# A planner that serializes the readers of one PSUM bank, with new leads for its transfers, in a linear attention joined to a gated MLP

## The chip, the cores and the metric

The kernel runs on one core of a Trainium2 chip. The core has five engines with a queue of instructions each: TensorE (PE in the rows; its weight loads are PEld), VectorE (DVE), ScalarE (ACT), GpSimd (POOL) and SyncE (SP), which here only starts DMA transfers. The metric is the device time of one execution in microseconds (us), the median of several.

## The reference

Two stages follow each other. For 4 batches, 8 heads, 768 steps and head size 48:

```python
for t in range(S):
    cur = einsum('bhd,bhe->bhde', u * k[t], v[t])
    y[t] = einsum('bhd,bhde->bhe', r[t], state + cur)
    state = w[t][..., None] * state + einsum('bhd,bhe->bhde', k[t], v[t])
# x = y as (3072 tokens, 384)
h = x @ w_in                       # 384 -> 2048
g = h if h >= 1, 0 if h <= -1, (h + 1)**2 / 4 between
out = g @ w_out                    # 2048 -> 384
```

All arrays are 32-bit floats.

## The kernel before, in words

The 3072 tokens are 12 units `u` of 256 tokens, and 6 blocks of two units (512 tokens). A unit's recurrence is done in chunks of 64 steps: VectorE scans the products of `w` forward (`p`, line 434) and backward (`y`, line 429), scales `r` and `k` with them, TensorE multiplies `r` with `k` inside the chunks (`among`, line 483), VectorE takes the wanted triangle of each product out of its PSUM bank with a mask (`picked`, line 489), TensorE transposes `k` (`ktrans`, line 522, into a bank that the masks must have left), forms the state updates (`umat`, line 544), VectorE adds them up (line 562), and TensorE forms the output in two PSUM banks, one for each half `g` of the unit (`cross` and `along`, line 593). From these banks the unit's `x` is taken in a high and a low part: ScalarE copies the high part (line 650), VectorE subtracts it from the bank to get the low part (line 648), first of three quarters (`x`), then of the last quarter (`last`), which six small DMAs then spread over free rows of `x` (`fill`, line 692). A unit of the first block takes its low part in another way (TensorE subtracts the high part in the bank, ScalarE copies what is left, line 646). For units from the fifth on, GpSimd makes the product of `r` and `k` of the diagonal (line 501) from a tile `nk` that has a transfer of its own.

The MLP runs over 16 slices `f` of 128 hidden columns for each block; the 16 slices' first 5 (block 0) or 11 (block 1) are done for each unit apart, so that they can start when one unit is there. A step is `product_in` (9 matmuls, line 944, into one of two banks `h`), the gate (ScalarE lines 755, 756 and 759, VectorE lines 757 and 760) and `product_out` (9 matmuls, line 964, added up in three banks `acc`). Weights come as raw bits (`wraw`), one transfer of 768 KB for each slice, and are decoded once: ScalarE (lines 355, 358), GpSimd (line 359, into the one buffer `rr`), VectorE (line 361), ScalarE for the high part (line 351), VectorE for the low part (line 364). At the end of a block the `acc` banks are copied out and stored. For each piece of `w` ScalarE also does two passes (`guard`, lines 711 and 712), whose result decides whether a general fallback runs; for the first six units `w` is loaded a second time for that, into `fl`.

What sets the order of everything is a planner in the kernel. Each operation is an entry with engine, cost, what it reads and writes, and a due time; `Plan.order` places the entries one after the other on the engines by these costs, and the instructions are emitted in that order. An attention unit or a weight decode is a group, whose entries are due a lead (`LEADS`, `DECODES`) plus `SLACK` times its remaining path ahead of the step that needs it. Each engine runs its queue strictly in the emitted order. Where the plan sees TensorE idle for over 0.5 us, `kept_warm` adds matmuls of zeros (line 326) for 0.72 of that gap.

The framework below adds its own waits between emitted instructions that touch the same tile on different engines.

Of the kernel before, what the change touches and what calls it, by code (L numbers as in the profile page):

```python
# [48 lines left out]
class Plan:  # L49
# [19 lines left out]
    def add(self, engine, cost, emit, due, reads=(), writes=(), port=False, size=0, fresh=True, mode=128):  # L69
        deps = {self.writer[x] for x in (*reads, *writes) if x in self.writer}  # L70
        for x in writes:
            deps.update(self.readers.get(x, ()))
        n = len(self.ops)
        for x in reads:
            self.readers.setdefault(x, []).append(n)
        for x in writes:
# [3 lines left out]
                             fresh=fresh and engine == "PE", touch={*reads, *writes}, mode=mode))  # L80
        return n

    def group(self, first, when, lead):

        tail = {}
        for n in reversed(range(first, len(self.ops))):
# [3 lines left out]
            op["due"] = when, lead + SLACK * tail[n]  # L90
# [39 lines left out]
    def order(self):  # L130
# [26 lines left out]
        while any(open_.values()):  # L157
# [57 lines left out]
SLACK = 1.384  # L215
LEADS = {0: 200.34, 1: 17.94, 2: 10.1, 3: 21.34, 4: 40.45, 5: 51.11, 6: 84.54, 7: 119.23, 8: 114.23, 9: 96.67, 10: 78.32, 11: 100.22}
DECODES = [58.08, 65.33, 175.35, 38.53, 1.42, 5.14, 81.19, 4.4, 14.07, 65.02, 61.72, 84.69, 39.36, 203.15, 25.09, -1.54]
LEAD = 15
# [12 lines left out]
STEP, FIRST, PACED, AFTER = 27.1568, 703.402, 25.4941, 4.9  # L231
# [3 lines left out]
def attention_moe(tc, a):  # L235
# [56 lines left out]
    def load(due, out, in_, writes, reads=()):  # L292
        size = 4
        for x in out.shape:
            size *= x
        return op("SP", 0.45, due, reads, writes, lambda: nc.sync.dma_start(out=out, in_=in_), size=size)
# [41 lines left out]
    def weight(f, when):  # L338
# [27 lines left out]
        plan.group(first, when, DECODES[f])  # L366
# [12 lines left out]
    def attention(u, when):  # L379
# [323 lines left out]
        plan.group(first, when, LEADS.get(u, LEAD))  # L703
# [33 lines left out]
    def products(n):  # L737
# [14 lines left out]
        op("PE", 0.16 + 2.11 * k, due, [("wh", f), ("wl", f), *xs], [("b", 6 + hk)],  # L752
# [13 lines left out]
        for terms in LAST if done else [TERMS]:  # L766
            op("PE", 0.16 + 2.11 * k * len(terms) / 9, due, [("gh", gk), ("gl", gk), ("wh", f), ("wl", f)],
# [38 lines left out]
    for n in range(2 * GUARDED):  # L806
# [3 lines left out]
        load(due, w, a["w"][u, q][:, 0:SEG], [("fl", n % 2)])  # L810
# [223 lines left out]
```

## Time and profile before

| | us |
|---|---|
| median of 3 runs (lowest, highest) | 514.54 (513.45, 517.81) |
| the profiled execution | 515.29 |
| its span, first to last instruction | 513.5 |
| PE busy | 495.0 (96% of the span) |
| DVE busy | 335.5 (65%) |
| ACT busy | 296.4 (58%) |
| POOL busy | 103.1 (20%) |
| DMA queue of SP | 53.21 MB, 30.5% of 16 engines |

The profiled execution is 1.8 us longer than its span. Busy time counts a matmul of zeros as work, and a matmul at a low clock as more work, so the 96% is no measure of what is left to gain; that is read from single stretches.

### The profile page before, as it was taken

Reading aid. Unit: us, or ns where it says so; the run is one execution under the profiler, and the core shown is the slowest. Engines: PE = TensorE matmul, PEld = TensorE weight load, DVE = VectorE, ACT = ScalarE, POOL = GpSimd, SP = SyncE. Lnnn points to the kernel's source line nnn. Section 1 sums busy time; section 2 is a strip of 40 time slices with the busy share of each in tenths; the row PEclk is TensorE's granted clock in tenths of the full one; section 3 lists DMA queues with packets and bytes.
Section 4 is the critical chain, followed back from the end, with each engine's and each line's share of the span. In section 5 each row is a group of like instructions: output and inputs, shape, how many; then the busy total and the mean of one; then the engine's idle time right before and its main releaser. Section 6 shows DMA issues by size and latency. Waiting matters only on the chain.

```text
span 513.5 us, 13078 instructions
## 1 busy us (share of the span) xinstructions
PE 495.0 (96%) x5558; PEld 414.1 (81%) x5558; DVE 335.5 (65%) x561; ACT 296.4 (58%) x604; POOL 103.1 (20%) x68
## 2 busy tenths in 40 slices
PE   8898999998999999999999999999999999999993
PEld 7778988786999987787888888888878888888883
DVE  7699997878997969799987567334552333333331
ACT  3478799968874665555556456443463444544441
POOL 2468858721022131112111020000100000000000
PEclk9899999998999999999999999999999999999997
DMA  8955644065751453264342050000120000100002
GB/s 319 391 217 206 213 176 173 2 225 171 235 144 64 152 191 103 76 220 144 91 135 82 21 182 6 1 0 3 57 75 6 0 1 1 63 0 0 1 0 68
DMA packets 21921, 54.11 MB, mean 105 GB/s; under 512 B 3104, under 2 KB 8672, under 8 KB 21856
## 3 DMA queue, kind: packets, MB, share of 16 engines
q1 hardware_dynamic: 21856, 53.21, 30.5%
q8 instruction: 45, 0.74, 0.6%
q14 instruction: 20, 0.16, 0.1%
HBM read 46.32 MB, written 4.72 MB: 99 GB/s over the span
## 4 chain that ended last, share of the span: by engine, by line
PE 70%; DVE 11%; ACT 6%; POOL 6%; issue 5%; DMA 2%; SPq 0%; POOLq 0%; DVEq 0%
PE acc L964 30%; PE h L944 29%; POOL rr L359 5%; PE bank L593 3%; PE bank L483 2%; DVE g L757 1%; PE bank L544 1%; PE bank L326 1%; PE bank L522 1%; DVE gl L760 1%; ACT g L756 1%; DVE fl L361 1%; DVE p L434 1%; DVE rk L463 1%; DVE rk L513 1%
## 5 line engine op out<-in xcount | busy, mean ns | idle before, releaser
L944 PE MATMUL h<-x,wt 128*128 128x512 f32 (+1 forms) x1008 | 216.2, 361 | 1.0 <-DMA x<-last 0.7
L944 PEld LDWEIGHTS h<-x,wt 128*128 128x128 f32 x1008 | 168.9, 188 | 30.7 <-DVE g L757 1.3
L964 PE MATMUL acc<-gh,wt 128*128 128x512 f32 (+1 forms) x672 | 153.1, 362 | 0.0
L964 PEld LDWEIGHTS acc<-gh,wt 128*128 128x128 f32 x672 | 113.8, 188 | 18.7
L757 DVE SCALAR_TENSOR_TENSOR g<-g,h 128x512 f32<-128x512 f32 (+1 forms) x112 | 67.8, 606 | 90.3 <-ACT g L756 86.3
L755 ACT ACTIVATE g<-h 128x512 f32<-128x512 f32 (+1 forms) x112 | 59.8, 534 | 79.2 <-PE h L944 73.9
L760 DVE TENSOR_TENSOR gl<-g,gh 128x512 fp32r<-128x512 f32 (+1 forms) x112 | 74.5, 667 | 36.6 <-ACT gh L759 35.6
L759 ACT CAST gh<-g 128x512 fp32r<-128x512 f32 (+1 forms) x112 | 62.1, 556 | 50.1 <-DVE g L757 49.3
L964 PE MATMUL acc<-gl,wt 128*128 128x512 f32 (+1 forms) x336 | 84.5, 359 | 0.0
L964 PEld LDWEIGHTS acc<-gl,wt 128*128 128x128 f32 x336 | 58.9, 189 | 9.7
L756 ACT ACTIVATE g<-g 128x512 f32<-128x512 f32 (+1 forms) x112 | 64.0, 571 | 3.2
L359 POOL TENSOR_SCALAR rr<-wraw 128x768 uint16<-128x768 f32 x16 | 53.3, 3331 | 33.6 <-DVE fl L361 20.4
L509 POOL TENSOR_TENSOR r<-cst,d 128x512 f32<-128x512 f32 x16 | 19.3, 1227 | 155.3 <-PE bank L593 126.5
L434 DVE TENSOR_TENSOR_SCAN p<-wq,seeds 128x514 f32<-128x514 f32 x24 | 33.0, 1373 | 4.1 <-POOL st L313 2.1
L429 DVE TENSOR_TENSOR_SCAN y<-wq,seeds 128x514 f32<-128x514 f32 x24 | 30.0, 1251 | 0.8
L501 POOL TENSOR_TENSOR nk<-nk 128x768 f32<-128x768 f32 x8 | 15.7, 1961 | 62.7 <-DMA nk<-in_nk 62.7
L463 DVE TENSOR_TENSOR rk<-rk,y 128x512 f32<-128x512 f32 x24 | 18.1, 755 | 5.9 <-ACT nk L454 3.1
L529 ACT COPY kt<-bank 128x512 f32<-128x512 f32 x24 | 14.0, 582 | 12.5 <-PE bank L522 12.5
L358 ACT ACTIVATE rr<-wraw 128x768 uint16<-128x768 uint32 x16 | 17.5, 1092 | 1.7 <-DMA wraw<-in_wbits 0.9
L326 PE MATMUL bank<-clear 128*128 128x512 f32 (+1 forms) x53 | 16.4, 431 | 1.6 <-DVE seeds L433 1.6
L513 DVE TENSOR_TENSOR rk<-rk,p 128x512 f32<-128x512 f32 x24 | 17.7, 751 | 0.2 <-PE acc L483 0.2
L593 PEld LDWEIGHTS bank<-rk,st 48*48 48x48 f32 (+1 forms) x656 | 11.5, 121 | 7.6 <-DVE st L562 2.2
(109 smaller groups left out, 393.6 us busy)
## 6 DMA issues: line engine op xcount, KB each, us to landing
rk<-in_rk SPq DMA_DIRECT2D x24, 512.0 KB, 5.3
wraw<-in_wbits SPq DMA_DIRECT2D x16, 768.0 KB, 7.1
wq<-in_w SPq DMA_DIRECT2D x24, 257.5 KB, 3.0
nk<-in_nk SPq DMA_DIRECT2D x8, 768.0 KB, 4.4
vn<-in_v SPq DMA_DIRECT2D x11, 384.0 KB, 6.0
fl<-in_w SPq DMA_DIRECT2D x12, 257.0 KB, 3.5
out_y<-g SPq DMA_DIRECT2D x11, 256.0 KB, 2.6
x<-last SPq DMA_DIRECT2D x66, 32.0 KB, 2.9
```

Of the source, the lines that this page charges most:

```text
L359: op("POOL", 3.35, due, [("raw", f)], ["rr_high"], lambda: G.tensor_scalar(out=r16[:, :, 1], in0=wraw[f][:, :, 1].bitcast(F32), scalar1=0. ...
L429: V.tensor_tensor_scan(out=y_[:, ::-1], data0=w[:, SEG:0:-1], data1=sv[:, ::-1], initial=0.0, op0=ALU.mult, op1=ALU.add)
L434: V.tensor_tensor_scan(out=pv[:, q].rearrange("p n c -> p (n c)"), data0=w[:, 0:SEG], data1=sv, initial=0.0, op0=ALU.mult, op1=ALU.add,)
L463: op("DVE", 0.69, due, ["y"], [("k", s)], lambda q=q: V.tensor_tensor(out=parts(q, 1), in0=parts(q, 1), in1=y_.rearrange("p (n c) -> p n c ...
L593: PE.matmul(out=bank[by[g]][HP * half : HP * half + wide, lo : lo + C], start=first, stop=False, skip_group_check=True, **kw)
L755: op("ACT", c, due, [("b", 6 + hk)], [("g", gk)], lambda: nc.scalar.activation(gs, hs, AF.Relu, scale=0.5, bias=0.5))
L756: op("ACT", c, due, (), [("g", gk)], lambda: nc.scalar.activation(gs, gs, AF.Square))
L757: op("DVE", 0.13 + 0.56 * k, due, [("b", 6 + hk)], [("g", gk)], lambda: nc.vector.scalar_tensor_tensor(out=gs, in0=gs, scalar=1.0, in1=hs, ...
L759: op("ACT", c, due, [("g", gk)], [("gh", gk)], lambda: nc.scalar.copy(ghs, gs))
L760: op("DVE", 0.18 + 0.52 * k, due, [("g", gk), ("gh", gk)], [("gl", gk)], lambda: nc.vector.tensor_tensor(out=gls, in0=gs, in1=ghs.bitcast( ...
L944: nc.tensor.matmul(by16(hp, f), lhsT=wx[f][:, cs], rhs=by16(xt[:, j, :], f), start=n == 0, stop=n == 8)
L964: nc.tensor.matmul(by16(o[j]), lhsT=wx[f][:, cs], rhs=by16(gt), start=first and i == 0, stop=stop and i == 2, skip_group_check=True)
```

## The change

Six things change. A reader of a PSUM bank now depends, in the plan, on all earlier readers of that bank on other engines. In the evacuation of `x`, ScalarE's copies of all high parts of a bank are planned first, and VectorE's low parts after them. Transfers over 32 KB of a group get a lead of their own, added to that of the group (`LOADS`, `RAWS`). The planned arrival of the second loads of `w` for the guards is 2.5 us later. The planned costs of a whole step's matmuls fall from 2.11 to 2.04. The tables and constants (`SLACK`, `LEADS`, `DECODES`, `AFTER`) have new values, and with all of this the order of nearly every queue is another one. No operation is added or removed except matmuls of zeros (55 matmul widths of 512 columns before, 58.5 now, counted in the order).

```diff
@@ Plan.add
+        for x in reads:
+            if isinstance(x, tuple) and x[0] == "b":
+                deps.update(m for m in self.readers.get(x, ()) if self.ops[m]["e"] != engine)
@@ Plan.group
-            op["due"] = when, lead + SLACK * tail[n]
+            op["due"] = when, lead + SLACK * tail[n] + (loads if op["e"] == "SP" and op["size"] > 32768 else 0.0)
@@ Plan.order
                 lands.append(end[n])
+                end[n] += op["spare"]
@@
-SLACK = 1.384
-LEADS = {0: 200.34, 1: 17.94, 2: 10.1, 3: 21.34, 4: 40.45, ...
+SLACK = 0.759
+LEADS = {0: 384.81, 1: 606.87, 2: 40.05, 3: 27.03, 4: 45.45, ...
+LOADS = {0: 9.57, 1: -384.0, 2: -5.47, 3: 9.66, 4: 7.78, ...
-STEP, FIRST, PACED, AFTER = 27.1568, 703.402, 25.4941, 4.9
+STEP, FIRST, PACED, AFTER = 27.1568, 703.402, 25.4941, 8.52
@@ weight
-        plan.group(first, when, DECODES[f])
+        plan.group(first, when, DECODES[f], RAWS[f])
@@ attention
-        for what in (0,) if alone else (1, 0):
+        whats = (0,) if alone else (1, 0)
+        for g in range(2):
+            for what in whats:
+                op("ACT", 0.27 if what else 0.48, due, [("b", by[g])], [names(what, 0, g)], lambda g=g, w=what: yevac(g, 0, w))
+        if u not in INPLACE:
             for g in range(2):
-                op("ACT", 0.27 if what else 0.48, due, [("b", by[g])], [names(what, 0, g)], lambda g=g, w=what: yevac(g, 0, w))
-                if u not in INPLACE:
+                for what in whats:
                     op("DVE", 0.27 if what else 0.54, due, [("b", by[g]), names(what, 0, g)], [names(what, 1, g)],
                        lambda g=g, w=what: yevac(g, 1, w))
@@ products
-        op("PE", 0.16 + 2.11 * k, due, [("wh", f), ("wl", f), *xs], [("b", 6 + hk)],
+        op("PE", 0.16 + (2.04 if f and k == 1.0 else 2.11) * k, due, [("wh", f), ("wl", f), *xs], [("b", 6 + hk)],
@@ second loads of w
-        load(due, w, a["w"][u, q][:, 0:SEG], [("fl", n % 2)])
+        load(due, w, a["w"][u, q][:, 0:SEG], [("fl", n % 2)], spare=2.5)
```

What the new order is like is seen at three places. The first is ScalarE's queue in the start, from the copies of the transposed `k` of unit 0 on; `look` and the copies `g<-acc` and `x<-acc` are unit 0's evacuation, `wraw`, `fl`, `rr` and `wt` belong to the decode of weights, `ptot<-p` and `nk<-rk` to unit 1. Before:

```order
L529 COPY kt_93<-bank_123 128x512
L355 ACTIVATE fl_115<-wraw_218 128x768
L629 COPY look_76<-acc_117 1x1
L629 COPY look_76<-acc_118 1x1
L358 ACTIVATE rr_116<-wraw_220 128x768
L673 COPY g_106<-acc_117 128x128
L673 COPY g_106<-acc_118 128x128
L355 ACTIVATE fl_114<-wraw_220 128x768
L460 COPY ptot_77<-p_88 128x2
L650 CAST x_101<-acc_117 128x3x128
L650 CAST x_101<-acc_118 128x3x128
```

And now:

```order
L534 COPY kt_93<-bank_123 128x512
L465 COPY ptot_77<-p_88 128x2 x2
L363 ACTIVATE rr_116<-wraw_229 128x768
L360 ACTIVATE fl_114<-wraw_229 128x768
L360 ACTIVATE fl_115<-wraw_276 128x768
L634 COPY look_76<-acc_117 1x1
L634 COPY look_76<-acc_118 1x1
L356 CAST wt_458<-fl_114 128x768
L678 COPY g_106<-acc_117 128x128
L678 COPY g_106<-acc_118 128x128
L363 ACTIVATE rr_116<-wraw_276 128x768
L360 ACTIVATE fl_114<-wraw_279 128x768
```

Two waits for unit 1's scans, the decode of weight 0 up to its high part and the first pass over weight 1 have moved ahead of unit 0's copies.

The second place is VectorE's queue at the same time; `r<-cst` and `r<-below` are the masks of unit 0, `ob`, `g` and `st` its states, `wq_81` is unit 1's `w`. Before:

```order
L513 TENSOR_TENSOR rk_83<-rk_83,p_88 128x512
L489 COPY_PREDICATED r_91<-cst_67,acc_117 128x512
L489 COPY_PREDICATED r_92<-cst_67,acc_118 128x512
L560 COPY ob_113<-h_121 128x4x48
L562 TENSOR_TENSOR ob_113<-bank_124,ob_113 128x4x48
L562 TENSOR_TENSOR g_106<-h_121,ob_113 128x4x48
L489 COPY_PREDICATED r_91<-below_71,acc_119 128x512
```

And now:

```order
L439 SCALAR_TENSOR_TENSOR p_88<-wq_81,seeds_73 128x514
L433 RECIPROCAL seeds_73<-p_88 128x2
L434 SCALAR_TENSOR_TENSOR y_89<-wq_81,seeds_73 128x514
L518 TENSOR_TENSOR rk_83<-rk_83,p_88 128x512
L438 MEMSET seeds_73 128x2
L439 SCALAR_TENSOR_TENSOR p_88<-wq_79,seeds_73 128x514
L565 COPY ob_113<-h_121 128x4x48
L567 TENSOR_TENSOR ob_113<-bank_124,ob_113 128x4x48
L494 COPY_PREDICATED r_91<-cst_67,acc_117 128x512
L494 COPY_PREDICATED r_92<-cst_67,acc_118 128x512
L567 TENSOR_TENSOR g_106<-h_121,ob_113 128x4x48
L494 COPY_PREDICATED r_91<-below_71,acc_119 128x512
```

Three scans of unit 1 (two forward, one backward) that stood behind unit 0's last mask now stand ahead of its first.

The third place is SP's queue at the end of block 0; `fl<-in_w` are the second loads of `w` for the guards, `nk<-in_nk` is the first tile from which GpSimd works on a diagonal, `out_y` block 0's results. Before:

```order
L692 DMA x_102<-last_103 16x2x256 x6
L296 DMA fl_115<-in_w 128x514
L296 DMA fl_114<-in_w 128x514
L296 DMA nk_85<-in_nk 128x1536
L296 DMA fl_115<-in_w 128x514
L296 DMA fl_114<-in_w 128x514
L296 DMA fl_115<-in_w 128x514
L296 DMA fl_114<-in_w 128x514
L296 DMA wq_81<-in_w 128x515
L778 DMA out_y<-g_105 128x512
```

And now:

```order
L700 DMA x_102<-last_103 16x2x256 x6
L301 DMA fl_114<-in_w 128x514
L301 DMA fl_115<-in_w 128x514
L301 DMA fl_114<-in_w 128x514
L301 DMA fl_115<-in_w 128x514
L301 DMA fl_114<-in_w 128x514
L786 DMA out_y<-ob_113 128x512
L786 DMA out_y<-g_105 128x512
L786 DMA out_y<-g_106 128x512
L301 DMA nk_85<-in_nk 128x1536
```

The `nk` tile, which was started between the second loads of `w`, now comes behind block 0's stores.

## Rows read from the trace of the kernel before

**Rows 1.** Stretches: us; busy PE, PEld, DVE, ACT, POOL (instructions); granted clock; DMA share; GB/s.

```profile
0.00:29.21 29.21, 25.39 (x531) 20.76 (x532) 21.03 (x35) 13.90 (x30) 9.12 (x22) 0.94 0.92 347
29.21:53.66 24.45, 21.80 (x439) 19.15 (x433) 24.01 (x41) 19.00 (x41) 20.81 (x9) 1.00 0.54 188
53.66:505.80 452.14, 447.81 (x4595) 374.20 (x4595) 290.05 (x486) 262.73 (x533) 73.21 (x38) 1.00 0.26 85
119.00:126.00 7.00, 5.01 (x67) 3.56 (x69) 6.49 (x10) 4.61 (x12) 0.48 (x1) 0.76 0.32 84
```

**Rows 2.** One of these stretches, matmuls of zeros (line 326) alone: us; busy PE, PEld.

```profile
53.66:505.80 452.14, 0.73 (x2) 0.30 (x2) 1.00 0.26 85
```

**Rows 3.** Timeline at 117 to 122 us; in brackets idle time before, and who ended it.

```profile
117.83 2.73 DVE L434 TENSOR_TENSOR_SCAN p<-wq,seeds 128x514 f32<-128x514 f32 x1
...
117.19 2.29 POOL L501 TENSOR_TENSOR nk<-nk 128x768 f32<-128x768 f32 x1 [7.95 <-DMA nk<-in_nk]
...
121.23 0.65 PE L522 MATMUL bank<-cst,rk 128*128 128x128 f32 x4 [1.99 <-DVE r L489]
```

**Rows 4.** Timeline at 200 to 207 us.

```profile
200.20 1.83 POOL L501 TENSOR_TENSOR nk<-nk 128x768 f32<-128x768 f32 x1 [8.35 <-DMA nk<-in_nk]
...
200.26 2.32 DVE L513 TENSOR_TENSOR rk<-rk,p 128x512 f32<-128x512 f32 x1
...
202.64 1.16 PE L483 MATMUL bank<-rk 64*64 64x64 f32 x64 [0.66 <-DVE seeds L433]
206.61 0.66 PE L522 MATMUL bank<-cst,rk 128*128 128x128 f32 x4 [0.58 <-DVE r L489]
```

**Rows 5.** Single lines: duration in ns, shortest, median and longest.

```profile
L434 DVE TENSOR_TENSOR_SCAN p<-wq,seeds x24: 1228/1229/2727, 3.6 to 312.2; 128x514 f32<-128x514 f32 x24
...
L513 DVE TENSOR_TENSOR rk<-rk,p x24: 665/684/2322, 10.8 to 364.4; 128x512 f32<-128x512 f32 x24
...
L501 POOL TENSOR_TENSOR nk<-nk x8: 1821/1846/2286, 117.2 to 280.0; 128x768 f32<-128x768 f32 x8
```

**Rows 6.** Timeline of the start, ACT, then DVE, then PE.

```profile
14.70 0.92 ACT L355 ACTIVATE fl<-wraw 128x768 f32<-128x768 f32 x1 [2.67 <-DMA wraw<-in_wbits]
...
16.62 1.07 ACT L358 ACTIVATE rr<-wraw 128x768 uint16<-128x768 uint32 x1 [0.91 <-DMA wraw<-in_wbits]
19.70 0.44 ACT L673 COPY g<-acc 128x128 f32<-128x128 f32 x2 [2.01 <-PE acc L593]
...
25.27 0.48 ACT L646 CAST x<-acc 128x384 fp32r<-128x384 f32 x1
...
15.11 0.71 DVE L489 COPY_PREDICATED r<-below,h 128x512 f32<-128x512 int32 x1
...
27.53 0.96 DVE L364 TENSOR_TENSOR wt<-fl,wt 128x768 fp32r<-128x768 f32 x1
...
18.12 0.27 PE L593 MATMUL acc<-rk,ob 48*64 48x64 f32 x1 [1.54 <-issue]
...
29.21 1.33 PE L944 MATMUL h<-x,wt 128*128 128x256 f32 x9
...
53.66 2.37 PE L944 MATMUL h<-x,wt 128*128 128x256 f32 x18 [0.72 <-DMA x<-last]
```

**Rows 7.** The decode of weights by line: count, busy us, mean ns, idle before.

```profile
L359 POOL TENSOR_SCALAR rr<-wraw 128x768 uint16<-128x768 f32 x16 | 53.3, 3331 | 33.6 <-DVE fl L361 20.4 <-DMA wraw<-in_wbits 13.1
...
L361 DVE SCALAR_TENSOR_TENSOR fl<-fl,rr 128x768 int32<-128x768 int32 x16 | 15.2, 951 | 2.7 <-POOL rr L359 2.6
...
L351 ACT CAST wt<-fl 128x768 fp32r<-128x768 f32 x16 | 13.2, 826 | 3.2 <-DVE fl L361 3.2
```

**Rows 8.** Who waited for whom, all of the span: us in total, times, longest.

```profile
ACT last L650 <- DVE x L648: 4.2, 7, 1.6
...
DVE x L648 <- ACT last L650: 3.7, 8, 0.5
```

**Rows 9.** The chain that ended last, in order of time: one `product_out` at 256 columns.

```profile
138.23 1.07 PE acc L964 x9
```

More of the change, by code (lines that the diff above doesn't have):

```diff
@@ L67, in __init__, with add @@
         self.ops, self.writer, self.readers = [], {}, {}
-    def add(self, engine, cost, emit, due, reads=(), writes=(), port=False, size=0, fresh=True, mode=128):
+    def add(self, engine, cost, emit, due, reads=(), writes=(), port=False, size=0, fresh=True, mode=128, spare=0.0):
         deps = {self.writer[x] for x in (*reads, *writes) if x in self.writer}
@@ L79, in add, with group @@
         self.ops.append(dict(e=engine, cost=cost, emit=emit, due=due, deps=deps, port=port, size=size,
-                             fresh=fresh and engine == "PE", touch={*reads, *writes}, mode=mode))
+                             fresh=fresh and engine == "PE", touch={*reads, *writes}, mode=mode, spare=spare))
         return n
-    def group(self, first, when, lead):
+    def group(self, first, when, lead, loads=0.0):
         tail = {}
@@ L211, in order @@
         return out
-SLACK = 1.384
-LEADS = {0: 200.34, 1: 17.94, 2: 10.1, 3: 21.34, 4: 40.45, 5: 51.11, 6: 84.54, 7: 119.23, 8: 114.23, 9: 96.67, 10: 78.32, 11: 100.22}
-DECODES = [58.08, 65.33, 175.35, 38.53, 1.42, 5.14, 81.19, 4.4, 14.07, 65.02, 61.72, 84.69, 39.36, 203.15, 25.09, -1.54]
-LEAD = 15
+SLACK = 0.759
+LEADS = {0: 384.81, 1: 606.87, 2: 40.05, 3: 27.03, 4: 45.45, 5: 71.8, 6: 60.98, 7: 25.74, 8: 81.18, 9: 211.42, 10: 77.25, 11: 123.12}
+DECODES = [100.35, 69.7, 39.12, 146.42, 32.88, 6.81, -6.35, -7.47, 249.78, -36.61, 27.78, -83.98, 25.56, 23.26, -16.63, -161.0]
+LOADS = {0: 9.57, 1: -384.0, 2: -5.47, 3: 9.66, 4: 7.78, 5: -12.47, 6: 37.12, 7: 0.0, 8: 6.52, 9: -48.34, 10: -46.8, 11: -16.85}
+RAWS = [0.0, -4.85, -25.68, 4.86, 33.83, -3.4, -2.07, 2.55, -2.88, 0.0, 79.29, 0.0, 0.0, 5.35, 18.51, -22.93]
 FLIGHT = 3
@@ L290, in op, with load @@
         return plan.add(engine, cost, emit, due, reads, writes, **kw)
-    def load(due, out, in_, writes, reads=()):
+    def load(due, out, in_, writes, reads=(), **kw):
         size = 4
@@ L295, in load @@
             size *= x
-        return op("SP", 0.45, due, reads, writes, lambda: nc.sync.dma_start(out=out, in_=in_), size=size)
+        return op("SP", 0.45, due, reads, writes, lambda: nc.sync.dma_start(out=out, in_=in_), size=size, **kw)
     SOON = 0, 200.0
@@ L702, in attention @@
                    lambda e=e, h=h, j=j: fill(e, h, j), size=32768)
-        plan.group(first, when, LEADS.get(u, LEAD))
+        plan.group(first, when, LEADS[u], LOADS[u])
         for q in range(2):
@@ L766, in products @@
         for terms in LAST if done else [TERMS]:
-            op("PE", 0.16 + 2.11 * k * len(terms) / 9, due, [("gh", gk), ("gl", gk), ("wh", f), ("wl", f)],
+            op("PE", 0.16 + (2.04 if k == 1.0 else 2.11) * k * len(terms) / 9, due, [("gh", gk), ("gl", gk), ("wh", f), ("wl", f)],
                sorted({("b", 3 + j) for _, j in terms}), fresh=begin,
```

## The prediction

> **What bounds the kernel now.** I read the table of stretches first [rows 1]. After 53.66 us, when the product of unit 1 starts, TensorE is busy for 447.81 of 452.14 us until its last matmul at 505.80; the 513.5 − 505.8 = 7.7 us behind that are copies and stores, which the change leaves alone. So from 53.66 us on TensorE is the bound, and a new order can only take back what it loses there: 452.14 − 447.81 = 4.33 us of idle time, 0.73 us of zeros [rows 2], and what a low clock costs. The clock fell in that part only at 119 to 126 us, where the mean granted clock is 0.76 and so some of the 7 us ran at 1.2 instead of 2.4 GHz: 7.00 × (1 − 0.76) = 1.7 us. Together 6.8 us. Ahead of 53.66 us the bound is the start: data must arrive, unit 0 and the first weights must be ready. There TensorE is idle for 29.21 − 25.39 = 3.8 us up to its first product, and 24.45 − 21.80 = 2.65 us behind it, and in this second stretch VectorE is busy for 24.01 of 24.45 us [rows 1].
>
> The idle time behind 53.66 us has two main places. At 119 us [rows 3] TensorE waits 1.99 us for VectorE's mask to free a bank for a transpose, because the scan ahead of the mask took 2.73 us where the median is 1.229 [rows 5], while GpSimd worked on `nk` from 117.19 to 119.48 us. After this wait the clock is low. At 200 us [rows 4] the same: a multiplication of VectorE takes 2.32 us where the median is 0.684 [rows 5], beside GpSimd's `nk` of 1.83 us, and TensorE then waits 0.66 and 0.58 us. So two chance meetings of VectorE with GpSimd cost 1.99 + 1.7 + 0.66 + 0.58 = 4.9 us.
>
> The Trainium skill (SBUF — State Buffer, section "Who interferes with whom") has this as a rule: a VectorE instruction with two SBUF inputs and a GpSimd instruction that reads SBUF take the same read port, and the one that starts second waits for the whole of the other. The rows agree: 2.32 us is GpSimd's 1.83 less the 0.06 of its head start, plus some 0.6. By that rule, which of the two wins depends on when a transfer of `nk` lands, and a plan that moves the transfer moves the meeting; it is not removed.
>
> **The change part by part.** *Meetings with GpSimd.* In the order, the first `nk` load leaves its place among the second loads of `w` and comes behind block 0's stores, so GpSimd's first 2.29 us can no longer fall on the scan ahead of those masks; the others shift as well. I take the whole 4.9 us as gone. But the eight `nk` operations [rows 5] remain, at new places, in a plan that again doesn't know when a transfer really lands. Before, eight of them cost TensorE 4.9 us, 0.6 each. The new plan has later loads and a longer planned time for the second loads of `w`; I take half of the old cost for new meetings and other unplanned waits, +2.5 us. Bounds: 0 (no meeting reaches TensorE) and +5 (as many as before).
>
> *Zeros.* After 53.66 us there were 0.73 us of zeros [rows 2]; in the order none stands there any more: −0.7 us. The other zeros stand in the start, where TensorE waits anyway.
>
> *The evacuation of `x`.* What moves is who waits. Before, VectorE's low part of a bank stood ahead of ScalarE's `last`, so ScalarE waited 4.2 us in all and VectorE 3.7 us [rows 8]. Now VectorE waits for both copies of its bank and ScalarE for nothing. That frees ScalarE for gates by 4.2 us over ten units, and delays VectorE's low parts by one short copy per bank. Neither is on TensorE's path after 53.66 us as long as a unit's `x` is ready some microseconds early; in the order at least five groups of nine matmuls at 512 columns, or eleven at 256, stand between the last output matmul of a unit from the third on and the product that needs it. I take 0, bounds −1 and +1.
>
> The Trainium skill (PSUM — Partial Sum Buffer, section "PSUM bank collisions raise a hardware error") says that ScalarE and VectorE must not touch one bank and quadrant at the same time, reads included, and that software keeps them apart. The waits in [rows 8] are such waits, so the plan before was counting on an overlap that it could not have. Going by the rule alone, the change would give the 4.2 us of ScalarE back to whatever waits for ScalarE; TensorE doesn't, so the sum is the same.
>
> *The start.* Here the order is most different, so I walk it. On VectorE three scans of unit 1 at 1.23 us each [rows 5], with their small instructions some 3.9 us, now stand ahead of unit 0's masks, whose last ended at 15.11 + 0.71 = 15.82 us [rows 6]. It will end at about 20.1 us, with 0.4 us for the `w` of unit 1 to land. The output matmuls that need the masks ran at 18.12 us, after 1.54 us of waiting that nothing in the profile explains [rows 6], so they come about 2.0 us later. On ScalarE the copies that follow them stood at 19.70 us. Now the high part of weight 0 stands ahead of them, which waits for VectorE's decode, 0.95 us [rows 7], behind the masks and two short operations on the states, so from some 20.8 us on; with its own 0.83 us [rows 7] the copies come at 22.5 us, 2.8 us later. Behind them ScalarE has three more decode passes (1.07, 0.92 and 0.83 us [rows 6, 7]) ahead of the last low part of `x`, which ended at 25.27 + 0.48 = 25.75 us and now ends at 25.75 + 2.8 = 28.5 us. But before, the first product did not wait for `x`: it waited for weight 0, whose low part ended at 27.53 + 0.96 = 28.49 us, and started at 29.21 us behind a product of unit 1. Now weight 0 is ready at about 23.5 us, so the first product starts at 28.5 us, 0.7 us sooner. Weights 1 to 4 are ahead of their old times too, since GpSimd, which takes 3.33 us for each and waited 20.4 us for VectorE's decodes [rows 7], takes weights 1 and 2, and not weight 1 alone, before its work for unit 2. Against that, unit 1's output comes later by the 2 to 3 us by which unit 0's evacuation came later on ScalarE and VectorE. The product of unit 1 (53.66 us before, after 0.72 us of waiting for the spread of `last`) so slips by about 1.3 us, but one more `product_out` (1.07 us [rows 9]) now stands ahead of it. I take 0 for the start. Bounds: −2 (the 0.7 and half of the 2.65 us of idle time behind the first product) and +5 (below).
>
> *The planned costs and `AFTER`* change no instruction; they are in the order already. In the steady part TensorE gets `product_out` somewhat later behind its `product_in`, which gives the gate more time: nothing to gain, since there is no wait.
>
> **The sum.** −4.9 + 2.5 − 0.7 + 0 + 0 = −3.1 us on the profiled execution's 515.29, 512.2; that execution is 0.75 above the median of the runs, so 511.4 is predicted as median (−0.6%). A measurement of this kernel can hardly tell less than 1%, 5.1 us, from no change.
>
> **The rivals.** *All waits go.* No `nk` operation meets a VectorE instruction on TensorE's path, and the start gains its 2 us: 514.54 − 4.9 − 0.7 − 2 = 506.9. By the skill's rule on the port this is what follows if the loads of `nk` land away from masks and scaling. For it: two of eight met before, so none of eight is not rare. Against it: VectorE is the busier engine in the start, where it gets three scans more ahead of the masks.
>
> *As many new waits as old ones.* The plan is another, its blindness the same; then the 4.9 us come back elsewhere, with a low clock behind one of them: 514.54 − 0.7 = 513.8. For it: no landing time is known to the planner. Against it: the long wait before needed a late ScalarE, a landing `nk` and a mask right behind.
>
> *The evacuation of unit 0 is held up by weights: slower.* On ScalarE two high parts of weights now stand ahead of parts of unit 0's evacuation. Each waits for GpSimd and VectorE, 3.33 + 0.95 = 4.3 us [rows 7] from the landing of its tile or the end of the decode before. I counted 2.8 us for both; if each takes its 4.3 us in full, 8.6 − 2.8 = 5.8 us more come ahead of the first product, less the 0.7 us that it is early: about +5. It decides against the change from the point where the first product starts later than 29.21 + 3.1 = 32.3 us: 514.54 − 3.1 + 5 = 516.4, and 519 with as many meetings as before. For it: ScalarE runs its queue in order, and before it already stood 2.67 and 0.91 us for weights that had not landed [rows 6]. Against it: ahead of weight 0 now stand four transfers of unit 1, 1411 KB by the shapes in the order, but no longer the 1536 KB of weights 1 and 2.
>
> *The change doesn't do what it says* is ruled out: the order shows all high parts ahead.
>
> **How the numbers follow.** Forecast 0.45, all waits go 0.27, as many new ones 0.13, slower 0.15. Faster by over 1% means below 509.4: the second case and a fifth of the first, less the second's upper end, 0.32. Slower by over 1% (above 519.7) is the outer half of the last, with some room for a wait that I don't see: 0.12. The rest, 0.56, is within 1%. The bounds give 514.54 − 2 − 1 − 4.9 − 0.7 = 505.9 and 514.54 + 5 + 1 − 5.6 + 5 = 519.9; with 2 in 10 left out I take 505.0 to 518.0, the lower end a little below since a low clock in the start (0.94 up to 29.21 us [rows 1]) may go as well.
>
> **What would show it.** Right: the scans and scalings at 115 to 125 and 198 to 208 us have their median durations, TensorE's idle time behind unit 1's first product is 2 to 3 us, the granted clock there is 1.00, and that product starts at 52 to 56 us. Wrong: a first product after 32 us; a new wait of TensorE of over 2 us with a low clock behind it; or TensorE waiting for the spread of `last` at the start of a block, which would mean that the units' new, later places have no room left.

## The result

| | us |
|---|---|
| before, median of 11 runs (lowest, highest) | 515.12 (512.07, 517.81) |
| after, median of 11 runs (lowest, highest) | 509.89 (507.67, 512.16) |
| ratio | 0.9899, 95% interval 0.9873 to 0.9926 |
| the profiled execution after, its span | 509.98, 508.1 |

The change makes the kernel 1% faster (0.7 to 1.3% by the interval). The time lies 1.5 us below the one predicted and inside the range. Most of this part shows that the reason given for it was not the one that holds.

Line numbers of the changed kernel, and of all experiments, are 5 to 8 higher: masks 494, `nk` 506, `ktrans` 527, output 598, evacuation 653 and 655, guard 719 and 720, gate 763 to 768, steps 952 and 972. The stretches of after, cut at the first product, unit 1's first product and the end of the matmuls, answer to [rows 1]:

```profile
0.00:27.04 27.04, 23.98 (x473) 19.14 (x474) 20.53 (x34) 13.60 (x29) 10.56 (x23) 1.00 0.96 360
27.04:52.78 25.74, 24.30 (x506) 21.34 (x505) 25.37 (x42) 21.45 (x45) 20.54 (x9) 1.00 0.56 193
52.78:500.50 447.72, 443.31 (x4585) 371.58 (x4584) 285.31 (x486) 259.44 (x530) 70.00 (x38) 1.00 0.26 86
```

The first product starts 2.2 us earlier, unit 1's 0.9 us earlier and behind one more `product_out`. Behind that the stretch is shorter (447.7 us for 452.1), the clock is 1.00 all the way, and no zeros are left in it, yet TensorE is idle for 447.72 − 443.31 = 4.41 us, as long as before (4.33). So it is TensorE's busy time that became shorter, by 447.81 − 443.31 = 4.5 us: 0.7 us of zeros, 1.7 us of low clock, 1.07 us of the `product_out` that now stands ahead, and some 1 us more. The mean over so long a stretch would hide some 3 us of low clock, as it does for before in [rows 1], but after has none between 6 and 504 us; that of the start (0.94 up to the first product in [rows 1]) is gone too. What TensorE waits for from 27 us on, in us in total, times and longest (the four longest in total):

```profile
PE bank L598 <- DVE st L567: 2.5, 4, 0.8
PE bank L488 <- DVE seeds L438: 1.3, 1, 1.3
PE h L952 <- DVE g L765: 0.7, 3, 0.3
PE bank L488 <- DVE rk L518: 0.7, 2, 0.4
```

Of these, 2.0, 1.3, 0.6 and 0.4 us lie behind 52 us. Two of the waits are new meetings of VectorE with GpSimd, which answer to [rows 3, 4]. The timeline of after at the two places (start, duration, then engine and instruction):

```profile
183.77 2.08 POOL L506 TENSOR_TENSOR nk<-nk 128x768 f32<-128x768 f32 x1 [10.08 <-DMA nk<-in_nk]
184.27 2.66 DVE L434 TENSOR_TENSOR_SCAN y<-wq,seeds 128x514 f32<-128x514 f32 x1
188.08 0.67 PE L598 MATMUL bank<-rk,st 48*48 48x64 f32 x32 [0.72 <-DVE st L567]
...
278.20 2.33 POOL L506 TENSOR_TENSOR nk<-nk 128x768 f32<-128x768 f32 x1 [8.87 <-DMA nk<-in_nk]
278.77 2.31 DVE L518 TENSOR_TENSOR rk<-rk,p 128x512 f32<-128x512 f32 x1
281.13 1.16 PE L488 MATMUL bank<-rk 64*64 64x64 f32 x64 [1.29 <-DVE seeds L438]
```

A scan takes 2.66 us and a scaling 2.31 us, beside `nk`, as before. Of the eight `nk`, five made a VectorE instruction at least 1.4 us longer before, three do now (the third, a scaling at 236.14 us, took 2.27 us). In both kernels TensorE came to wait behind two of them.

**Lost time.** Two kernels whose TensorE does things in another order can't be compared time by time. So I worked out a number from each trace: at the start of the n-th of the 112 `product_in`, the time less the work that TensorE had done by then (each matmul counted with the mean spacing of its shape in one run, zeros with nothing). Each row is a single execution, up to 2.2 us off the median of its kernel (guards_later 516.88 for 519.05), so the table tells where time is lost, and the medians how much a kernel takes. Only differences mean something, and between two orders with some care: the spacing is a little short for the small matmuls of the attention, so a stretch with many of them shows up to 1.3 us that are no wait. Product 6 is unit 1's first, 21 the last of block 0 (105 to 111 us), 25 lies at 124 to 132 us.

```
lost us at product      6    21    25    45   last matmul
before               26.9  28.1  33.0  34.5  40.6
after                24.9  27.4  27.4  27.8  35.9
new_start            25.4  28.1  31.5  34.3  40.4
old_start            28.3  32.6  32.6  33.1  39.1
before_new_evac      26.7  27.9  29.2  31.0  37.0
after_old_evac       24.5  27.0  27.0  29.4  35.6
scan_behind_masks    26.2  27.4  32.3  35.1  40.9
before_no_nk         27.2  28.4  32.3  34.6  38.8
after_no_nk          25.2  27.7  27.8  28.2  33.5
after_nk_four        25.3  27.6  27.6  28.4  32.9
guards_later         26.2  27.3  29.6  36.5  42.2
evac_nk_four         25.0  26.2  28.3  30.1  34.7
guards_evac_nk       26.9  28.0  30.4  38.1  43.0
guards_spread_nk     28.9  30.1  31.3  34.4  42.8
```

Before to after, the start gains 2.0 us at product 6, of which 0.7 are left at product 21. Then comes the place that matters: between products 21 and 25 the kernel before loses 4.9 us, the changed one nothing. Of the 4.9, 3.7 are the wait of 1.99 us and the 1.7 us of low clock of [rows 1, 3]; the rest is attention, which the changed kernel does later (it loses 8.5 us behind product 25, before 7.6). In the changed kernel TensorE has no wait in this part (columns as in [rows 1]):

```profile
107.00:132.00 25.00, 25.00 (x396) 22.27 (x396) 15.96 (x32) 20.43 (x51) 1.85 (x1) 1.00 0.47 141
```

So the question is what the 3.7 us at 107 to 132 us hang on.

### The profile page after: what moved, and what is told of

Read it like the earlier page. It is cut to its first block, busy times and chain, and to the rows that moved or that the text cites. A ratio compares the mean times of both kernels' runs of the same rounds, so it can differ in the third digit from the quotient of the medians.

```text
span 508.1 us, 13247 instructions
## 1 busy us (share of the span) xinstructions
PE 492.1 (97%) x5562; PEld 412.2 (81%) x5562; DVE 332.0 (65%) x561; ACT 295.4 (58%) x604; POOL 101.1 (20%) x68
## 4 chain that ended last, share of the span: by engine, by line
PE 76%; DVE 13%; ACT 3%; DMA 3%; issue 3%; SPq 1%; DVEq 0%; ACTq 0%
PE h L952 34%; PE acc L972 33%; PE bank L598 4%; DVE y L434 2%; DVE r L494 2%; PE bank L488 2%; DVE wt L369 2%; DMA rk<-in_rk 1%; DVE p L439 1%; PE bank L527 1%; DMA wq<-in_w 1%; PE bank L549 1%; DVE g L765 1%; DVE gl L768 1%; DVE rk L518 1%
## 5 line engine op out<-in xcount | busy, mean ns | idle before, releaser
L768 DVE TENSOR_TENSOR gl<-g,gh 128x512 fp32r<-128x512 f32 (+1 forms) x112 | 71.4, 642 | 28.6 <-ACT gh L767 13.4
L514 POOL TENSOR_TENSOR r<-cst,d 128x512 f32<-128x512 f32 x16 | 18.0, 1145 | 159.4 <-PE bank L598 134.0
L506 POOL TENSOR_TENSOR nk<-nk 128x768 f32<-128x768 f32 x8 | 16.9, 2108 | 80.3 <-DMA nk<-in_nk 71.2
L434 DVE TENSOR_TENSOR_SCAN y<-wq,seeds 128x514 f32<-128x514 f32 x24 | 32.2, 1342 | 0.8
L439 DVE TENSOR_TENSOR_SCAN p<-wq,seeds 128x514 f32<-128x514 f32 x24 | 30.2, 1259 | 3.5 <-POOL st L318 2.1
L369 DVE TENSOR_TENSOR wt<-fl,wt 128x768 fp32r<-128x768 f32 x16 | 16.4, 1032 | 3.2 <-ACT wt L356 3.1
```

The lines of the kernel that those rows point to most:

```text
L369: op("DVE", 0.95, due, [("fl", k), ("wh", f)], [("wl", f)], lambda: V.tensor_tensor(out=w_lo[f], in0=s, in1=w_hi[f].bitcast(F32), op=ALU.s ...
L434: V.tensor_tensor_scan(out=y_[:, ::-1], data0=w[:, SEG:0:-1], data1=sv[:, ::-1], initial=0.0, op0=ALU.mult, op1=ALU.add)
L439: V.tensor_tensor_scan(out=pv[:, q].rearrange("p n c -> p (n c)"), data0=w[:, 0:SEG], data1=sv, initial=0.0, op0=ALU.mult, op1=ALU.add,)
L768: op("DVE", 0.18 + 0.52 * k, due, [("g", gk), ("gh", gk)], [("gl", gk)], lambda: nc.vector.tensor_tensor(out=gls, in0=gs, in1=ghs.bitcast( ...
```

## The experiments

All are built on the changed kernel's code, with the planner's loop replaced by a list of its entries (a number is an entry, a pair a filler of zeros), so that any order can be given:

```diff
-        for emit in plan.kept_warm(plan.best(step_ops, dues), "PE", [("b", i) for i in range(8)], zeros):
-            emit()
+        for n in ORDER:
+            plan.ops[n]["emit"]() if isinstance(n, int) else zeros(("b", n[0]), n[1])
```

With the list of the kernel before, this gives its queues row by row. The theory at first was the prediction's: meetings with `nk` and the start. The rivals were the evacuation, and one stretch alone. Ratios are to the kernel before on the same chip, with 95% intervals. The median of before was 513.9 to 514.9 us there.

### The start and the rest, apart: new_start, old_start

```diff
-ORDER = before
+ORDER = after[:after.index(409)] + [n for n in before if n not in after[:after.index(409)]]
```

Entry 409 is the first product over both units, product 11, at 63 to 67 us. The expectations name unit 1's first product as the cut, which lies some 11 us earlier; the cut was at 409. old_start has before and after changed about.

> Every queue has the changed kernel's order up to the first product of unit 1, and the order of the kernel before from there on. My theory: the start gains some 2 us by itself (first product of unit 1 at 52 to 53 us with one more output step done), the rest keeps its long wait of VectorE with GpSimd and the low clock behind it, so 515.1 - 2.0 = 513.1 us (ratio 0.996). Rival A, the start gives all of the gain because later waits follow from it: 509.9 (0.990). Rival B, what the start gains is given back later, since the next unit is not ready sooner: 515.1 (1.000), with a wait of TensorE of about 2 us between 53 and 110 us.

> The counterpart: the order of the kernel before up to the first product of unit 1, the changed kernel's from there on. My theory: the zeros and the low clock go (0.7 + 1.7 us and about 0.8 of other small things), the start stays: 515.1 - 3.2 = 511.9 us (0.994). Rival A: 515.1 (1.000), the long wait at 119 us is back or another stands in its place. Rival B: 509.9 (0.990), all of the gain is behind 53 us.

Measured: new_start 514.44 us, 0.9997 (0.9967 to 1.0026); old_start 513.58 us, 0.9977 (0.9950 to 1.0004). Alone, the new start is worth nothing that the interval tells from zero (−1.7 to +1.3 us): its 1.5 us at product 6 are gone at product 21 (28.1 for 28.1), since VectorE's gates come late for it (TensorE waits for `g` 0.9 us in all between 53 and 110 us). Rival B holds for it. The new rest behind the old start is not worth its 3.2 us either: it loses 4.3 us between products 6 and 21, with this wait of TensorE

```profile
87.01 0.67 PE L598 MATMUL bank<-rk,st 48*48 48x64 f32 x32 [1.78 <-DVE st L567]
```

and a granted clock of 0.94 in the stretch around it (columns as in [rows 1]):

```profile
66.79:95.00 28.21, 25.95 (x294) 20.97 (x293) 22.78 (x32) 24.17 (x40) 17.10 (x6) 0.94 0.48 180
```

But between products 21 and 25 it loses nothing, as the changed kernel. The two halves don't add up to the whole; the order is one plan.

new_start also says something of the meeting at 119 us. ScalarE waits its 1.6 us for `last` there as before, but `nk` lands later, so that the scan (117.56 us, 1.23 us long) is ahead of it (118.86 us). There is no meeting and no low clock, and still 3.4 us are lost between products 21 and 25.

### The meeting at 119 us alone: scan_behind_masks

In VectorE's queue of the kernel before (and ScalarE's copy `ptot` from this scan likewise):

```diff
-MEMSET seeds
-TENSOR_TENSOR_SCAN p<-wq,seeds
 COPY_PREDICATED r<-below,bank
 SCALAR_TENSOR_TENSOR g<-g,h
 COPY_PREDICATED r<-below,bank
+MEMSET seeds
+TENSOR_TENSOR_SCAN p<-wq,seeds
```

> The kernel before, with one thing moved: the forward scan of unit 4 that met GpSimd's product at 117.8 us (and ScalarE's small copy from it) comes behind the two masks of unit 3 instead of ahead of them. My theory: the wait of 1.99 us and the 1.7 us of low clock behind it go, 515.1 - 3.7 = 511.4 us (0.993). Rival A, the scan is missed later and the wait comes back in another place: 515.1 (1.000). Rival B, the clock falls there whatever TensorE waits for: 515.1 - 2.0 = 513.1 (0.996).

Measured: 514.46 us, 0.9995 (0.9965 to 1.0025). The theory fails: the masks are free of the scan, and as much is lost (4.9 us between products 21 and 25) as before. The timeline:

```profile
118.87 1.83 POOL L506 TENSOR_TENSOR nk<-nk 128x768 f32<-128x768 f32 x1 [11.03 <-DMA nk<-in_nk]
119.28 2.50 DVE L439 TENSOR_TENSOR_SCAN p<-wq,seeds 128x514 f32<-128x514 f32 x1
...
121.82 0.19 ACT L465 COPY ptot<-p 128x2 f32<-128x2 f32 x1 [0.97 <-DVE p L439]
122.76 0.56 ACT L534 COPY kt<-bank 128x512 f32<-128x512 f32 x1
...
123.38 1.53 PE L549 MATMUL bank<-vn,kt 64*48 64x48 f32 x64 [2.34 <-ACT kt L534]
```

The scan meets `nk` again, and now TensorE waits 2.34 us for ScalarE's copy of the transposed `k`, which stands behind two guard passes (one waited 0.77 us for `fl`) and the copy from the scan. So next to VectorE's late masks ScalarE was late too. Since the scan met `nk` again, this run doesn't show what the meeting alone costs; the next ones do.

### No meetings at all: before_no_nk, after_no_nk, after_nk_four

```diff
-                out=nk[:, :, 0, :], in0=nk[:, :, 0, :], in1=nk[:, :, 1, :], op=ALU.mult), port=True)
+                out=nk[:, :, 0, 0:1], in0=nk[:, :, 0, 0:1], in1=nk[:, :, 1, 0:1], op=ALU.mult), port=True)
```

and for after_nk_four four instructions of 192 columns:

```diff
+            op("POOL", 2.2, due, (), ["nk"], lambda: [G.tensor_tensor(out=nk[:, i, 0, c:c + 192], in0=nk[:, i, 0, c:c + 192],
+                in1=nk[:, i, 1, c:c + 192], op=ALU.mult) for i in range(2) for c in (0, 192)], port=True)
```

> The kernel before, but GpSimd's eight products nk work on one column of each half instead of all 384 (the diagonal terms of units 4 to 11 are so left out of the result); transfers and all else stay. My theory: no meeting is left, the waits of 1.99, 0.66 and 0.58 us and the low clock go: 515.1 - 4.9 = 510.2 us (0.9905). Rival, the long scan and scaling have another cause than GpSimd and stay: 515.1 (1.000).

> The changed kernel with the same cut of GpSimd's eight products nk to one column of each half (diagonal terms of units 4 to 11 left out). My theory: its two waits behind meetings, 0.72 and 1.29 us, go: 509.9 - 2.0 = 507.9 us (0.986). Rival, they are replaced by waits for the next link of the chain: 509.9 (0.990). With the cut in both kernels, what is left between them (510.2 to 507.9) is the start's 2 us.

> The changed kernel, GpSimd's products nk in four instructions of 192 columns each instead of one of 768. My theory, an instruction of VectorE waits for the instruction of GpSimd under way: a meeting then costs at most a quarter, 0.5 us, and the two waits of 0.72 and 1.29 us nearly go: 508.2 us (0.987). Rival A, VectorE waits for all four: 509.9 (0.990). Rival B, GpSimd's share grows by overhead and later meetings are hit: 511 (0.992).

Measured: before_no_nk 512.54 us, 0.9956 (0.9932 to 0.9979); after_no_nk 507.78 us, 0.9860 (0.9825 to 0.9895); after_nk_four 507.21 us, 0.9861 (0.9824 to 0.9898). The meetings cost the kernel before 514.91 − 512.54 = 2.4 us (1.1 to 3.5 by the interval), not 4.9, and the changed one 509.89 − 507.78 = 2.1 us. So they are worth nearly the same in both, and without them the change is still worth 0.9860 / 0.9956 = 0.9904, all that it is worth with them; the two intervals leave some 0.4%, 2 us, of doubt in this. In before_no_nk no scan is long and the clock stays at 1.00 there, and still 3.9 us are lost between products 21 and 25, 1.0 less than before. Its timeline there:

```profile
117.85 1.23 DVE L439 TENSOR_TENSOR_SCAN p<-wq,seeds 128x514 f32<-128x514 f32 x1
...
121.00 0.64 ACT L719 ACTIVATE fl<-fl 128x514 f32<-128x514 f32 x1 [1.70 <-DMA fl<-in_w]
123.22 0.56 ACT L534 COPY kt<-bank 128x512 f32<-128x512 f32 x1
...
123.84 0.94 PE L549 MATMUL bank<-vn,kt 64*48 64x48 f32 x64 [1.39 <-ACT kt L534]
```

ScalarE stands 1.70 us for a second load of `w`, and TensorE then 1.39 us for the copy behind it. What the meetings cost before came at 200 us [rows 4]: 1.5 us between products 45 and 49 are gone.

The four pieces do as well as no `nk` at all. In after_nk_four the first of the two meetings shown above has become:

```profile
183.26 4.26 POOL L506 TENSOR_TENSOR nk<-nk 128x192 f32<-128x192 f32 x4 [9.12 <-DMA nk<-in_nk]
184.01 1.02 DVE L468 TENSOR_TENSOR rk<-rk,y 128x512 f32<-128x512 f32 x1
185.15 1.43 DVE L434 TENSOR_TENSOR_SCAN y<-wq,seeds 128x514 f32<-128x514 f32 x1
```

The scan takes 1.43 us instead of 2.66; GpSimd's four now wait for VectorE in between, 4.26 us in all, for which no engine waits here. It is the fastest kernel of the study that computes everything: five of its six runs are at most 507.94 us, of the changed kernel's eleven one is, though the two intervals still overlap.

### The evacuation alone: before_new_evac, after_old_evac

The emitted order of a unit's evacuation (ACT high parts, DVE low parts), for the ten units with low parts on VectorE:

```diff
 ACT CAST x<-bank of half 0
 ACT CAST x<-bank of half 1
-DVE TENSOR_TENSOR x<-bank of half 0, x
 ACT CAST last<-bank of half 0
 ACT CAST last<-bank of half 1
+DVE TENSOR_TENSOR x<-bank of half 0, x
 DVE TENSOR_TENSOR x<-bank of half 1, x
```

> The kernel before in its own order, only that in the evacuation of x ScalarE's copies of a unit are written ahead of VectorE's low parts, for the ten units where VectorE makes these. ScalarE's queue is the same as before, VectorE's has four low parts later in two units. My theory: ScalarE's 4.2 us of waiting go, VectorE waits instead, TensorE feels neither: 515.1 within 1 us (0.998 to 1.002). Rival, the waits of ScalarE were what put VectorE late for its masks and scalings: 512 us or less (below 0.994).

> The changed kernel in its own order, only that the first low part of VectorE stands ahead of ScalarE's copies of the last quarter again, as in the kernel before, in ten units. My theory: ScalarE waits some 4 us in all again and the time stays: 509.9 within 1 us (0.988 to 0.992). Rival, the new evacuation carries the gain: 513 us or more (over 0.995).

Measured: before_new_evac 513.03 us, 0.9955 (0.9925 to 0.9984); after_old_evac 511.53 us, 0.9939 (0.9914 to 0.9964). The theory fails for the first: with the instructions of ScalarE's queue unchanged, 1.3 instead of 4.9 us are lost between products 21 and 25, and the last matmul comes 3.7 us earlier in the profile; by the ratio it is 0.45%, 2.3 us. The stretch of 107 to 132 us (columns as in [rows 1]) of the kernel before:

```profile
107.00:132.00 25.00, 23.01 (x395) 18.91 (x393) 20.38 (x33) 19.28 (x46) 4.53 (x3) 0.93 0.60 190
```

and of before_new_evac, where TensorE has no wait in it:

```profile
107.00:132.00 25.00, 25.00 (x426) 21.89 (x425) 20.54 (x37) 20.97 (x52) 3.94 (x3) 1.00 0.70 215
```

For the second the interval overlaps the changed kernel's (0.9873 to 0.9926), so 1.6 us slower by the medians is likely and not settled.

The chain shows in ScalarE's and SP's rows of the kernel before, which the prediction does not use:

```profile
102.78 0.86 ACT L650 CAST x<-bank 128x384 fp32r<-128x384 f32 x2 [0.67 <-PE bank L593]
105.23 0.43 ACT L650 CAST last<-bank 128x128 fp32r<-128x128 f32 x2 [1.59 <-DVE x L648]
114.55 0.64 ACT L711 ACTIVATE fl<-fl 128x514 f32<-128x514 f32 x1 [1.35 <-DMA fl<-in_w]
116.46 0.60 ACT L759 CAST gh<-g 128x512 fp32r<-128x512 f32 x1
...
106.73 3.78 SPq L692 DMA_DIRECT2D x<-last  x6
110.61 1.91 SPq L296 DMA_DIRECT2D fl<-in_w  x2
```

and in the same places of before_new_evac:

```profile
103.35 0.46 ACT L655 CAST last<-bank 128x128 fp32r<-128x128 f32 x2
113.20 0.64 ACT L719 ACTIVATE fl<-fl 128x514 f32<-128x514 f32 x1 [0.49 <-DMA fl<-in_w]
115.11 0.60 ACT L767 CAST gh<-g 128x512 fp32r<-128x512 f32 x1
...
105.95 3.78 SPq L700 DMA_DIRECT2D x<-last  x6
109.82 1.44 SPq L301 DMA_DIRECT2D fl<-in_w  x2
...
116.49 1.23 DVE L439 TENSOR_TENSOR_SCAN p<-wq,seeds 128x514 f32<-128x514 f32 x1
116.88 2.48 POOL L506 TENSOR_TENSOR nk<-nk 128x768 f32<-128x768 f32 x1 [8.42 <-DMA nk<-in_nk]
```

Before, ScalarE waits 1.59 us for VectorE's low part ahead of `last`. So the six small transfers start later, by 0.78 us, and behind them in SP's queue the second loads of `w`; for these ScalarE's guard pass then waits 1.35 us, and the gate's cast behind the passes is at 116.46 us. VectorE's low part of the gate waits for the cast, and the scan behind it starts at 117.83 us, 0.64 us after `nk` [rows 3]. With the new evacuation the scan starts at 116.49 us, ahead of `nk`, and it is GpSimd that waits (2.48 us). So the meeting at 119 us hung on ScalarE's delay, and on when `nk` landed: with the same delay new_start has no meeting.

### The guards out of the way: guards_later, guards_spread_nk

In both, the loads of `fl` and ScalarE's passes are moved as a group in the order of the kernel before: 40 places later (as below, ScalarE's queue), or spread over 440 places behind block 0 and with `nk` in four.

```diff
-ACTIVATE fl<-fl 128x514
-ACTIVATE fl,above<-fl,minus_one 128x514
-ACTIVATE fl<-fl 128x514
 CAST gh<-g 128x512
...
 COPY kt<-bank 128x512
+ACTIVATE fl<-fl 128x514
```

> The kernel before, with one thing moved: the second loads of w for the guards and ScalarE's two passes over each (all but the first load and pass) stand 40 places later in the emitted order, so that both copies of the transposed k of unit 3 come ahead of them. My theory by now: between 100 and 131 us ScalarE's queue is the late link. It waits 1.59 us for VectorE's low part ahead of the last quarter, SP's six small transfers follow 1.1 us late, the second loads of w behind these land late, ScalarE's guard pass waits 1.35 us for them, and the copies and casts behind it, and then VectorE's scan, are late, so that the scan comes just behind GpSimd's nk. With the guards out of the way ScalarE isn't late: 515 - 3.5 = 511.5 us (ratio 0.993), and no wait of over 1 us at 115 to 125 us. Rival A, the wait for the last quarter acts without the guards, through the six transfers or through VectorE: 515 (1.000). Rival B, the guards now stand ahead of unit 3's six transfers in SP's queue and hold up its product: 517 (1.004).

> The kernel before with the old evacuation, GpSimd's nk in four instructions, and eleven of the twelve second loads of w with ScalarE's guard passes spread over the emitted order behind both evacuations of block 1, one every 40 places, each load 20 places ahead of its passes, so that ScalarE never stands for one and they stand in nobody's way. To be compared with the kernel before whose nk was cut (512.5 us, 0.9956), where ScalarE waited 4.6 us in all for these loads and TensorE 1.4 us for a copy of the transposed k behind them. My theory, these waits are the link from ScalarE's late queue to TensorE between 107 and 131 us: what was lost there beyond the changed kernel, 4 us, mostly goes: 512.5 - 3 = 509.5 us (0.990). Rival, the old evacuation's wait makes ScalarE late with or without guards, and TensorE waits for the same copy: 512.5 (0.9956). Second rival, the guards passes now collide with the gates of later blocks: 513 or more (0.997), with new waits of TensorE for ScalarE behind 160 us.

Measured: guards_later 519.05 us, 1.0114 (1.0070 to 1.0158); guards_spread_nk 515.43 us, 1.0008 (0.9984 to 1.0033). Both totals miss my theory. At the place in question it holds: between products 21 and 25, 2.3 and 1.2 us are lost instead of 4.9, with the old evacuation; in guards_later TensorE has no wait between 109 and 123 us, in guards_spread_nk none between 107 and 132. What is gained is paid back elsewhere. In guards_later the passes crowd ahead of unit 3, ScalarE stands 2.88 us for `fl` there, and TensorE waits 2.11 us for its cast (the 1.65 us ahead of that are for VectorE):

```profile
139.58 0.63 ACT L719 ACTIVATE fl<-fl 128x514 f32<-128x514 f32 x1 [2.88 <-DMA fl<-in_w]
141.19 0.39 ACT L767 CAST gh<-g 128x256 fp32r<-128x256 f32 x1
...
135.62 1.33 PE L952 MATMUL h<-x,wt 128*128 128x256 f32 x9 [1.65 <-DVE seeds L438]
141.63 0.97 PE L972 MATMUL acc<-gh,wt 128*128 128x256 f32 x6 [2.11 <-ACT gh L767]
```

So the guards in ScalarE's queue are shown twice as the link, once by their absence and once at a new place. How much of it is the standing for `fl` and how much the passes' own time (some 1.5 us for each piece of `w`) no run tells apart. In guards_spread_nk 7 us are lost between products 45 and 65, for 2.8 in before_no_nk; there `nk` in four meets three VectorE instructions in a row (1.08, 1.07 and 1.48 us for 0.68, 0.68 and 1.23), and TensorE waits 1.37 us. This accounts for part of it only.

### Put together in the old order: evac_nk_four, guards_evac_nk

The list of before_new_evac, and that with the guards of guards_later, both with `nk` in four.

> The order of the kernel before with the new evacuation of x (as in the run with that alone, 0.9955) and GpSimd's nk in four instructions. My theory: the new evacuation already takes away the meeting at 119 us, so the four pieces add only what the meeting at 200 us costs, about 1.4 us: 515 - 1.9 - 1.4 = 511.7 us (0.9935). Rival A, both gains overlap in full: 513 (0.9955). Rival B, the two effects are all that the change is worth, and the order counts for nothing: 507.5 (0.986), as the changed kernel with four pieces.

> All three in the order of the kernel before: the guards 40 places later, the new evacuation, nk in four. My theory: guards and evacuation take away the same wait, so this is the better of both with 1.4 us for nk: 510 to 511.5 us (0.991 to 0.993). Rival A, they add up: 508 (0.987). Rival B, the guards in unit 3's way cost what they gain: 512 or more (over 0.995).

Measured: evac_nk_four 510.29 us, 0.9938 (0.9912 to 0.9964), as expected, though the interval takes in rival A's 0.9955; guards_evac_nk 517.57 us, 1.0086 (1.0056 to 1.0115), rival B. So two small edits take the old order to within some 0.8% of after_nk_four, which is what the new order itself is worth beside them.

## Why the prediction was right or wrong

The number was right by luck, with a sum that was not: a term too large by 2.5 us (4.9 for 2.4) stood in for one of about that size that the sum lacked, ScalarE's delay.

**The step that failed** is "So two chance meetings of VectorE with GpSimd cost 1.99 + 1.7 + 0.66 + 0.58 = 4.9 us". I took the wait that TensorE named, and the long instruction ahead of it, for the cause. scan_behind_masks and before_no_nk show that at 119 us VectorE and ScalarE were late side by side: with the meeting taken away, 2.6 of the 3.7 us stay lost (3.9 less the 1.3 that before_new_evac shows there without a wait), and with the scan moved, where it met `nk` again, all of them. The meeting at 200 us was sized well (1.24 us of waits; 1.5 us gone in before_no_nk). The term is 2.4 us, with 1.1 to 3.5 as its interval.

**New meetings, +2.5 us:** 2.1 us by after_no_nk. For the meetings, mechanism and size were right. The term was to hold other unplanned waits too, and with these TensorE is idle for 4.41 us behind unit 1's first product, as long as before. Net, the meetings are worth −0.3 us, not −2.4.

**The evacuation, 0 with bounds −1 and +1:** wrong. Alone it gives some −2.3 us in the old order (0.9955). The step was "Neither is on TensorE's path after 53.66 us as long as a unit's `x` is ready some microseconds early". I asked only who waits for `x`, and not what else stands behind the waiting ScalarE: its guard passes, and behind SP's six transfers the loads that these need. [Rows 8] had the 4.2 us; the prediction does not ask where they fell.

**The start, 0 with bounds −2 and +5:** product 6 comes with 2.0 us less lost, the lower bound, and the walk was close up to ScalarE's copies: the last mask of unit 0 ended at 19.88 us (20.1 predicted), ScalarE's copies came at 22.15 (22.5), the first product at 27.04 (28.5). The product of unit 1 came at 52.78 us, where the walk had it slip by 1.3 us from 53.66, so there it was 2 us off. But alone the start is worth nothing in the end that shows (0.9997, 0.9967 to 1.0026), so 0 was the right entry, though not for my reason.

**The planned costs, zeros −0.7, the clock:** the zeros are gone, and the clock is 1.00 from 52.78 us up to the last matmul. The low clock at 119 us went too; in before_no_nk it is gone as well, with 1.39 us for the longest wait, but other waits stand in its place there.

**What was missing** is ScalarE's delay at 107 to 132 us, the 2.6 us of before_no_nk and more than half of the 512.54 − 507.78 = 4.8 us that the change is worth without meetings. The rest are the 0.7 us of zeros, the 0.7 us that the start keeps up to product 21, and small waits that I did not tell apart. The evacuation or the guards' place each take most of the delay away in the old order. In the changed kernel unit 2's six transfers start at 93.92 us instead of 106.73, the loads of `fl` only from 101.35 us on, and ScalarE waits for none of them from 90 to 126 us:

```profile
93.92 3.78 SPq L700 DMA_DIRECT2D x<-last  x6
101.35 13.38 SPq L301 DMA_DIRECT2D fl<-in_w  x5
```

That this is why nothing is lost there, even with the old evacuation (27.0 and 27.0), is argued from these rows; no run moved unit 2 alone.

**The rivals.** "All waits go", 506.9 us, is what after_nk_four reaches (507.21), but with an edit that the change does not have; and "two of eight met before" was too low, since five of the eight met. "As many new waits as old ones" was right about the waits (4.41 us idle for 4.33, meetings worth 2.1 us for 2.4) and wrong in its time, 513.8, because the kernel gained elsewhere. "Slower" decided at a first product after 32.3 us; it came at 27.04.

**What would show it:** normal scans at 115 to 125 and 198 to 208 us, a clock of 1.00 and unit 1's product at 52.78 us were as said; 2 to 3 us of idle time behind it were not (4.41).

The Trainium skill (SBUF — State Buffer, section "Who interferes with whom") says that the port is held for a whole instruction, and that the order of issue decides who blocks. The runs agree on both: a scan that starts 0.5 us behind `nk` takes 2.66 us, one that starts 0.4 us ahead of it takes 1.23 and `nk` 2.48; and pieces of 0.6 us bring the scan down to 1.43.

**Open:** what the evacuation is worth in the new order (1.6 us by medians whose intervals overlap; in its one profile the last matmul ends no later, at 500.80 us for 501.04, and the longer span lies behind it), and why guards_spread_nk lost all of 7 us between products 45 and 65.

## What to carry to other kernels

The instruction that a stalled engine waits for is the end of a chain, and there may be a second chain just as late: before a stall is put into a sum, look at what each of the other queues was doing in the 15 us ahead of it, above all at in-order queues that stood for something unimportant (here a check's data, behind six small transfers, behind a copy). Two readers of one PSUM bank on different engines are put in series by the order in which they are written, so which comes first is a choice with a price. Where a GpSimd instruction shares VectorE's port and its start hangs on a transfer, it can be cut into pieces: in after_nk_four no VectorE instruction lost more than some 0.4 us to it, wherever they met. Several in a row can still add up, as the 1.0 us over three in guards_spread_nk.

## What the runs showed of the hardware

Part of the scatter of one kernel's time goes with its meetings. Without them the changed kernel's six runs lie within 0.8 us (507.16 to 507.96), with them eleven runs within 4.5 us (507.67 to 512.16), and six with `nk` in four within 2.0 us (507.06 to 509.09). The kernel before keeps 3.5 us of scatter without them (511.12 to 514.64). In the profiles its start is part of it: at product 6 the runs with the old start have lost 25.0 to 28.9 us, those with the new one 24.5 to 25.4. The 1.54 us at 18 us that TensorE stood for nothing that the profile shows [rows 6] belong to the old order of the start: all nine traces with it have such a wait of 1.46 to 1.99 us at 18 to 20 us, and none of the five with the new start has one. In one of the nine (guards_spread_nk) TensorE stood another 2.04 us at 34 us. The cause of both stays open.

GpSimd's other instruction holds VectorE too: in after_old_evac a forward scan at 152.41 us took 1.95 us beside the product for the diagonal (line 514). Of the sixteen of these, none of my terms spoke.
